# Block-sparse attention with a gated feed-forward: edge rows copied on chip, weights loaded behind the first inputs, squares added on GpSimd, fill matmuls, and new ranks

## The chip, the cores and the metric

The kernel runs on one core of a Trainium2 chip. The metric is the device time in microseconds (us), smaller is better. A core has five engines that run their own rows of instructions in order and wait for one another by semaphores: TensorE (PE in the profile, its weight loads apart as PEld), VectorE (DVE), ScalarE (ACT), GpSimd (POOL) and SyncE (SP, which here only issues transfers).

## The reference

Attention for 4 batches of 8 heads, 768 rows of 64 numbers each, and then a gated feed-forward over all 3072 tokens. Attention is sparse by blocks of 32 rows: a block of queries sees itself and its two neighbours, the first and the last block (the edge blocks), and three sampled blocks; the first and the last block of queries see all keys.

```python
scores = scale * np.matmul(q, k.transpose(0, 1, 3, 2))
mask = np.abs(blk_i - blk_j) <= window
mask = mask | (blk_i == 0) | (blk_j == 0) | (blk_i == n_blocks - 1) | (blk_j == n_blocks - 1)
...
        mask[qb * block:(qb + 1) * block, kb * block:(kb + 1) * block] = True
...
attn = attn / (np.sum(attn, axis=-1, keepdims=True) + 1e-09)
return np.matmul(attn, v).astype(np.float32)
```

```python
g = x @ w_gate
silu = g * (1.0 / (1.0 + np.exp(-g)))
val = x @ w_val
return (silu * val @ w_out).astype(np.float32)
```

Here x has 3072 rows of 512, w_gate and w_val are 512 x 1536, w_out is 1536 x 512.

## The kernel before

**Tiles and chunks.** A tile is four query blocks, 128 tokens; a batch has six. Tiles are grouped into nine chunks: three of two tiles (batch 0) and six of three tiles (batches 1 to 3). For each chunk the attention of its tiles writes x transposed into `xall`, and then `ffn_in` makes the hidden rows h, and `ffn_out` the output rows.

**Batch 0 and the weights.** The weights come as 64-bit words, in pieces of 512 KB, into four slots of `stage` (L453). VectorE turns two of them at a time into float32 by three passes (L431 to L433). Chunks 0 and 1 use those float32 weights (the "wide" projections, L1687). Meanwhile ScalarE and VectorE split each weight into two float16 halves (L391 and L394), and all later projections (`p`, L1693) and output matmuls (`po`, L1754) use three float16 products.

Batch 0's attention is worked in pairs of query blocks (`pair0`). A pair gathers its keys into `kring`, its values into a slot of `w2all`: window rows by copies from the resident v of batch 0 (L1315, on VectorE or ScalarE), sampled rows by an indirect transfer (L1319, issued by GpSimd), and edge rows, which four broadcast loads (L606) put once into all six slots, by `e0_done`. Then come scores (`qk`, L1338 and L1354), maxima on VectorE (`mx`, L1360), exponentials on ScalarE (`e`, L1371), transposes on TensorE (`pt`, L1379) with copies out (`pts`, L1385), the product with the values (`pv`, L1400), scaling (`xs`, L1408), a transpose back (L1417), and a copy into `xall` (L1464).

**The norm of a chunk.** `ffn_in` scales its hidden rows by a bound for the norm of x: ScalarE squares x (`sqx`, L1632) in four blocks of the chunk's tokens, four matmuls on a matrix of ones add them up over blocks and partitions (`xn`, L1637), and VectorE makes scales from it (L1641).

**What sets the order.** Nothing is ordered by hand. Each step is a task of a planner (`Plan.add`) with an engine, a cost in us, the tasks it needs, the buffers it takes, and a rank. `Plan.order` plays the tasks through: an engine that is free takes the task with the lowest rank of those that are ready and whose buffers are free by the planner's own clock. `queue` and `lanes` model the transfers. The ranks get an addition by key from the table `SHIFT`, thousands either way, so the table sets the order in fact. The tasks are then emitted in that order, so each engine's row is fixed when the program is built. `behind` puts a task behind another on its queue; `first_loads` chains the first loads on SP's queue. SP uses eight lanes for its transfers: a ninth waits for the one eight before it.

Of the kernel before, what the change touches and what calls it, by code (L numbers as in the profile page):

```python
# [13 lines left out]
ALU = mybir.AluOpType  # L14
AX = mybir.AxisListType

P = 128
B, H, S, D = 4, 8, 768, 64
BLK = 32
# [24 lines left out]
LANES = 8  # L44


SHIFT = {
# [72 lines left out]
class Plan:  # L120
# [9 lines left out]
    def add(self, eng, us, emit, need=(), rank=0.0, take=(), use=(), dma=None, behind=None, late=0.0, many=1):  # L130
# [8 lines left out]
        if behind is not None:  # L139
            behind.next.append(t)  # L140
# [87 lines left out]
def tile_block_sparse_attn_swiglu(  # L228
# [381 lines left out]
    def more_v0(rank):  # L610
        for i in range(1, 3):
            batches[0].v0_part(i, rank)
# [1240 lines left out]
```

## Time and profile before

Times are the median of three runs, 798.54 us (798.23 to 799.63). The profile shows one execution of its own.

| what | value |
|---|---|
| profiled execution | 799.88 us |
| its span, first to last instruction | 798.1 us |
| TensorE busy | 758.0 us (95%) |
| VectorE busy | 548.9 us (69%) |
| ScalarE busy | 507.5 us (64%) |
| GpSimd busy | 208.3 us (26%) |
| mean granted clock of TensorE | 0.991 |
| moved by transfers | 128.08 MB |

How to read it: the page gives the busy time of each engine and the span in 40 slices. The timeline lists instructions with start, duration and, in brackets, how long the engine was idle before and what released it. A row may stand for several instructions (x16). The table of stretches gives each engine's busy time between two points of the span; the stretch's length less that is the engine's idle. Idle time of an engine matters only where it holds up what ends last.

### The profile page before, as it was taken

Reading aid. Unit: us, or ns where it says so; the run is one execution under the profiler, and the core shown is the slowest. Engines: PE = TensorE matmul, PEld = TensorE weight load, DVE = VectorE, ACT = ScalarE, POOL = GpSimd, SP = SyncE. Lnnn points to the kernel's source line nnn. Section 1 sums busy time; section 2 is a strip of 40 time slices with the busy share of each in tenths; the row PEclk is TensorE's granted clock in tenths of the full one; section 3 lists DMA queues with packets and bytes.
Section 4 is the critical chain, followed back from the end, with each engine's and each line's share of the span. In section 5 each row is a group of like instructions: output and inputs, shape, how many; then the busy total and the mean of one; then the engine's idle time right before and its main releaser. Section 6 shows DMA issues by size and latency. Waiting matters only on the chain. (4 is left out here: it accounts for less than half of the span.)

```text
span 798.1 us, 21157 instructions
## 1 busy us (share of the span) xinstructions
PE 758.0 (95%) x8062; PEld 482.3 (60%) x8062; DVE 548.9 (69%) x1662; ACT 507.5 (64%) x1232; POOL 208.3 (26%) x257
## 2 busy tenths in 40 slices
PE   3689999999999999999999999999999999999998
PEld 2468778874687566645665566545665566555653
DVE  5688898997898696742799757654798767731320
ACT  2699657688688686754588746664497757642211
POOL 3466302322043232102233232301223233101210
PEclk9799999999999999999999999999999999999999
DMA  8965547558787977677779994947878974430001
GB/s 203 258 215 177 184 158 235 198 145 215 182 179 170 216 164 160 125 212 215 159 170 177 259 245 95 182 103 206 187 141 185 222 170 110 65 74 14 1 1 39
DMA packets 171286, 128.08 MB, mean 160 GB/s; under 512 B 114992, under 2 KB 136624, under 8 KB 171184
## 3 DMA queue, kind: packets, MB, share of 16 engines
q1 hardware_dynamic: 165552, 109.42, 57.2%
q0 software_dynamic: 5632, 17.31, 8.7%
q8 instruction: 63, 1.03, 0.6%
q14 instruction: 39, 0.32, 0.1%
HBM read 79.50 MB, written 11.01 MB: 113 GB/s over the span
## 5 line engine op out<-in xcount | busy, mean ns | idle before, releaser
L1693 PE MATMUL p<-xall,w1t 128*128 128x384 f16 (+1 forms) x2016 | 326.8, 319 | 0.0
L1693 PEld LDWEIGHTS <-w1t 128*128 128x128 f16 x2016 | 191.1, 98 | 116.1 <-issue 9.0
L1715 POOL TENSOR_TENSOR h<-act,h 128x384 f16<-128x384 f32 (+1 forms) x108 | 101.1, 937 | 375.7 <-ACT h L1712 375.4
L1754 PE MATMUL po<-w2all,h 128*128 128x512 f16 x864 | 195.2, 379 | 0.3 <-DVE w2all L394 0.3
L1754 PEld LDWEIGHTS <-h 128*128 128x128 f16 x864 | 81.0, 98 | 97.0 <-issue 5.7
L1121 POOL DMA_INDIRECT w2all<-vd,vidx x66 | 64.9, 983 | 150.3 <-PE pv L1203 127.6
L1702 DVE SCALAR_TENSOR_TENSOR act<-act,p 128x384 f32<-128x384 f32 (+1 forms) x108 | 54.2, 503 | 68.2 <-ACT act L1698 67.6
L1712 ACT CAST h<-act 128x384 f16<-128x384 f32 (+1 forms) x108 | 50.6, 470 | 78.5 <-DVE act L1707 78.2
L1687 PE MATMUL p<-xall,w1t 128*128 128x256 f32 x384 | 88.2, 383 | 1.3 <-DVE act L1702 1.3
L1165 ACT ACTIVATE e<-e,nb,es 128x256 f32<-128x256 f32 x132 | 78.2, 593 | 2.2
L1687 PEld LDWEIGHTS p<-xall,w1t 128*128 128x128 f32 x384 | 70.8, 190 | 12.7 <-DVE act L1702 1.9
L1698 ACT ACTIVATE act<-p,gsc 128x384 f32<-128x384 f32 (+1 forms) x84 | 46.9, 558 | 31.8 <-PE p L1693 31.3
L1203 PEld LDWEIGHTS <-w2all 128*128 128x128 f16 x1584 | 55.0, 98 | 16.1 <-issue 6.4
L1707 DVE SCALAR_TENSOR_TENSOR act<-act,hs,p 128x384 f32<-128x384 f32 (+1 forms) x84 | 49.6, 590 | 20.3 <-PE p L1693 17.7
L394 DVE SCALAR_TENSOR_TENSOR pp<-e,rr,pp 128x256 f16<-128x256 f32 x132 | 61.1, 510 | 1.3 <-ACT pp L391 1.0
L1203 PE MATMUL pv<-pts,w2all 128*128 128x64 f16 x1584 | 57.0, 193 | 4.6 <-DMA pts<-pp 3.2
L391 ACT ACTIVATE pp<-e,rr 128x256 f16<-128x256 f32 x132 | 58.1, 496 | 4.4 <-DVE rr L779 2.8
L1148 DVE CUSTOM_DVE_ANT_1 e<-qk,msk 128x256 f32<-128x256 f32 x132 | 49.9, 417 | 3.1 <-issue 2.7
L1593 ACT ACTIVATE ot<-po,oc 128x512 f32<-128x512 f32 x24 | 16.4, 683 | 44.1 <-PE po L1754 43.9
L1111 DVE COPY kring<-kst 128x256 f16 x198 | 38.7, 251 | 6.3 <-PE qk L1134 6.3
L1229 DVE TENSOR_TENSOR xall<-pv,xall 64x256 f16<-64x256 f32 x66 | 27.7, 420 | 21.1 <-ACT xall L1224 20.0
L1134 PE MATMUL qk<-kring,qs 128*32 128x256 f16 x1056 | 35.7, 274 | 0.8 <-DVE mx L1148 0.6
(189 smaller groups left out, 899.1 us busy)
## 6 DMA issues: line engine op xcount, KB each, us to landing
stage<-in_w_dram SPq DMA_DIRECT2D x36, 512.0 KB, 4.4
w2all<-vd SPq DMA_DIRECT2D x66, 192.0 KB, 3.9
qs<-qraw SPq DMA_DIRECT2D x72, 128.0 KB, 2.4
out_dram<-ot SPq DMA_DIRECT2D x20, 256.0 KB, 2.7
qn<-in_q_dram SPq DMA_DIRECT2D x36, 128.0 KB, 4.0
qraw<-in_q_dram SPq DMA_DIRECT2D x36, 128.0 KB, 3.1
stage<-in_v_dram SPq DMA_DIRECT2D x9, 512.0 KB, 5.3
vd<-stage SPq DMA_DIRECT2D x9, 512.0 KB, 5.9
```

Source lines behind the costliest of these rows:

```text
L391: nc.scalar.activation(hi, src, AF.Copy, scale=scale)
L394: nc.vector.scalar_tensor_tensor(lo, src, scale, hi, op0=ALU.mult, op1=ALU.subtract)
L1121: nc.gpsimd.indirect_dma_start(vf[0:96, 1, :], None, bt.vd, bass.IndirectOffsetOnAxis(ap=vidx[0:96, qb : qb + 1], axis=0))
L1148: nc.vector.tensor_tensor_reduce(ev[:, g], stv[:, g], o.g.msk[:, qb, :].unsqueeze(2).broadcast_to([P, 8, BLK]), scale=1.0, scalar=-3.0e38, ...
L1165: nc.scalar.activation(ev[:, g], ev[:, g], AF.Exp, bias=nb_[:, g : g + 1], scale=o.g.es[:, 0:1], accum_out=c["rs"][:, g : g + 1],)
L1203: nc.tensor.matmul(pvv[:, j, n % 2], vg[:, cc, l, 2 * j : 2 * j + 2, :], pq[:, g, m, cc, u : u + 2, :], start=i == 0, stop=i == 5,)
L1687: nc.tensor.matmul(t[:, 0:tc_], w[:, i + 1, k_ * P : (k_ + 1) * P], x_k(k_), start=k_ == 0, stop=k_ == NKT - 1)
L1693: nc.tensor.matmul(t[:, 0:tc_], w_[:, f, m, k_, :], x_k(k_, l), start=i == 0, stop=i == 11)
L1702: nc.vector.scalar_tensor_tensor(a_, a_, 1.0, pg.tile[:, 0:tc_], op0=ALU.add, op1=ALU.mult)
L1712: nc.scalar.copy(hv(f)[:, 0, :], act.tile[:, 0:tc_])
L1715: nc.gpsimd.tensor_tensor(hv(f)[:, 1, :], act.tile[:, 0:tc_], hv(f)[:, 0, :], op=ALU.subtract)
L1754: nc.tensor.matmul(po.tile, hv(f)[:, l, ts_], w2h[:, f, m, :], start=f == 0 and i == 0, stop=f == NF - 1 and i == 2)
```

## The change

Seven edits go together.

- The four broadcast loads of edge rows go. `edges` copies the first and the last 32 rows of v into the slots on chip: four copies of 32 x 512 on ScalarE, four of 32 x 1024 on VectorE. A pair's product needs the copies of its own slots (`edge_of`) in place of all four loads. The last part of v is loaded directly behind the first, the middle one later.
- Weight loads are chained behind the last of the first loads, not behind the seventh.
- The four blocks of squares are added on GpSimd, two on two and then one on one (`add_up`), and one matmul on ones is left of four.
- 83 tasks of four matmuls of ones by ones, 128 x 128 (`keep_on`), with rank 9000, so that the planner takes them when TensorE has nothing else that is ready. They write into the ring of buffers `pv`.
- The planner's prices: transfers start at 3.9 in place of 2.0 us, the table has no `late`, and early TensorE tasks get the price of later ones.
- Query loads and their spreading are chained in order (`q_last`).
- A new table `SHIFT`, with keys for the new copies.

```diff
+DMA_START = 3.9
...
-    "a0.0": 215.65, "a0.1": -2208.54, "a1.0": 2743.2, "a1.1": -905.98, "a2.0": -5449.96, "a2.1": 1137, "a3.0": -2069.74,
+    "a0.0": 2014.17, "a0.1": -1926.27, "a1.0": 1312.03, "a1.1": 3189.83, "a2.0": 3082.71, "a2.1": 1535.27, "a3.0":
...
-        a = add("SP", 0.37, lambda: load(0), need, rank, take=raw, behind=first_loads[6], dma=1.7)
+        a = add("SP", 0.37, lambda: load(0), need, rank, take=raw, behind=first_loads[-1], dma=1.7)
...
         part(0, rank)
-        for m in range(2):
-            sl = slice(0, BLK) if m else slice(96, P)
-            for n, r0 in enumerate((0, S - BLK)):
-                e0_done.append(first(add("SP", 0.45, lambda m=m, sl=sl, n=n, r0=r0: nc.sync.dma_start(
-                    w2all[sl, n + 2 * m : 2 * V0_RING : 4, :],
-                    v[0, r0 : r0 + BLK, :].unsqueeze(1).broadcast_to([BLK, V0_RING // 2, DM])), [], rank, behind=first_loads[-1], dma=0.8)))
+        part(2, rank)
+
+    def edges(x, n, k, eng, us, rank):
+
+        sl = slice(0, BLK) if x % 2 else slice(96, P)
+        src = w2t[96:P, V0_AT + NTB - 1, :] if n else w2t[0:BLK, V0_AT, :]
+
+        def copy():
+            f = nc.vector.tensor_copy if eng == "DVE" else nc.scalar.copy
+            f(w2all[sl, 2 * x + n : 2 * x + n + 4 * k - 3 : 4, :], src.unsqueeze(1).broadcast_to([BLK, k, DM]))
+
+        plan.key = f"e{x}.{n}"
+        t = add(eng, us, copy, [batches[0].v0_loads[2 * n]], rank)
+        batches[0].v0_read.append(t)
+        for i in range(x, x + 2 * k, 2):
+            edge_of[i].append(t)
+
+    def all_edges(rank):
+        for x in range(2):
+            for n in range(2):
+                edges(x, n, 1, "ACT", 0.62, rank)
+        for x in range(2, 4):
+            for n in range(2):
+                edges(x, n, 2, "DVE", 0.7, rank + 0.5)
...
-        a = in_turn("pv", "PE", 1.06 if ci else 1.8, product, there + vl + e0_done, rank, take=[pv], use=pts)
+        a = in_turn("pv", "PE", 1.06, product, there + vl + [t for x, _ in vb for t in edge_of[x]], rank, take=[pv], use=pts)
...
-            for j in range(4):
-                nc.tensor.matmul(t[:, 0:tc_], ones_h, sq_view()[:, j], start=j == 0, stop=j == 3)
+            nc.tensor.matmul(t[:, 0:tc_], ones_h, sq_view()[:, 0], start=True, stop=True)
+
+        def add_up(n):
+            x = sq_view()
+            nc.gpsimd.tensor_tensor(x[:, 0:n], x[:, 0:n], x[:, n : 2 * n], op=ALU.add)
...
-        a = add("PE", nt * 0.22, norms, [a], rank - 1000.0, take=[xn], use=[sq])
+        a = add("POOL", 0.64 * nt, lambda: add_up(2), [a], EVAC, use=[sq])
+        a = add("POOL", 0.32 * nt, lambda: add_up(1), [a], EVAC, use=[sq])
+        a = add("PE", nt * 0.055, norms, [a], rank - 1000.0, take=[xn], use=[sq])
...
+    def keep_on(n, us):
+        plan.key = ""
+
+        def turn_over(w):
+            t = get(w, "idle")
+            for _ in range(4):
+                nc.tensor.matmul(t[:, 0:P], ones_h, ones_h, start=True, stop=True)
+
+        for _ in range(n):
+            w = Buf("pv")
+            add("PE", us, lambda w=w: turn_over(w), [t_id], 9000.0, take=[w])
...
+    keep_on(8, 0.43)
+    keep_on(75, 0.21)
     load_k0(K0)
```

In the changed program the 332 fill matmuls stand on TensorE as follows: 100 ahead of the first transposes of k, 28 between them, 60 behind them and ahead of the first scores, and 144 between scores, transposes and products of the pairs up to the sixth.

On SP's queue at the start of the program, before: query tile 0 (`q_0`), the first part of v, the edge rows (32x3x512), a weight piece (`stage`), query tile 1, and the rest.

```order
L1265 DMA q_0_132<-in_q_dram 64x4x128 x2
L597 DMA w2all<-in_v_dram 128x2x512
L606 DMA w2all<-in_v_dram 32x3x512 x4
L453 DMA stage<-in_w_dram 128x1024
L1265 DMA q_0_132<-in_q_dram 64x4x128 x2
L597 DMA w2all<-in_v_dram 128x2x512 x2
L453 DMA stage<-in_w_dram 128x1024 x3
L1265 DMA q_1_459<-in_q_dram 64x4x128 x4
```

The same place on SP's queue now:

```order
L1289 DMA q_0_147<-in_q_dram 64x4x128 x2
L600 DMA w2all<-in_v_dram 128x2x512 x2
L1289 DMA q_0_147<-in_q_dram 64x4x128 x2
L600 DMA w2all<-in_v_dram 128x2x512
L1289 DMA q_1_473<-in_q_dram 64x4x128 x4
L456 DMA stage<-in_w_dram 128x1024 x4
```

The edge loads are gone, the second query tile moved ahead of one v part and of the first weight piece, and chunk 1's queries (`q_1`) ahead of all weights.

On ScalarE's row behind the copies of k's transposes, where it first needs v, before: window copies into `w2all`, the squares of v (`vsq`), then the exponentials of the first pair (`nb_1`, `e_1`).

```order
L1315 COPY w2all<-w2all 96x512
L1315 COPY w2all<-w2all 64x512
L1315 COPY w2all<-w2all 32x512
L398 ACTIVATE vsq_361,vacc_360<-w2all 128x1024
L1315 COPY w2all<-w2all 96x512
L1369 ACTIVATE nb_1_0_419<-mx_1_376 128x2
L1371 ACTIVATE e_1_0_417,rs_1_416<-qk_1_0_321,nb_1_0_419 128x256 x2
```

The same place on ScalarE's row now, with the edge copies (L615):

```order
L615 COPY w2all<-w2all 32x512
L401 ACTIVATE vsq_589,vacc_588<-w2all 128x1024
L615 COPY w2all<-w2all 32x512 x2
L401 ACTIVATE vsq_589,vacc_588<-w2all 128x1024
L1393 ACTIVATE nb_1_0_679<-mx_1_626 128x2
L1395 ACTIVATE e_1_0_677,rs_1_676<-qk_1_0_549,nb_1_0_679 128x256 x2
L1339 COPY w2all<-w2all 96x512
```

Three edge copies and a second part of v's squares, which needs the second v load, moved ahead of the first pair's exponentials, and the window copies behind them.

On GpSimd's row near the end, where the last chunk's h begins (`h_0`), before: the last differences of the chunk before it, and then those of the last chunk.

```order
L1715 TENSOR_TENSOR h_8_11627<-act_9_11652,h_8_11627 128x384
L1715 TENSOR_TENSOR h_10_11762<-act_10_11723,h_10_11762 128x384
L1715 TENSOR_TENSOR h_10_11762<-act_11_11813,h_10_11762 128x384
L1715 TENSOR_TENSOR h_0_12209<-act_0_12192,h_0_12209 128x384
L1715 TENSOR_TENSOR h_0_12209<-act_1_12225,h_0_12209 128x384
```

The same place on GpSimd's row now:

```order
L1744 TENSOR_TENSOR h_8_12076<-act_9_12107,h_8_12076 128x384
L1744 TENSOR_TENSOR h_10_12257<-act_10_12195,h_10_12257 128x384
L1744 TENSOR_TENSOR h_10_12257<-act_11_12313,h_10_12257 128x384
L1664 TENSOR_TENSOR sqx_12490<-sqx_12490 128x768
L1664 TENSOR_TENSOR sqx_12490<-sqx_12490 128x384
L1744 TENSOR_TENSOR h_0_12619<-act_0_12602,h_0_12619 128x384
```

The two adds of squares stand between the two chunks' differences, and TensorE's one norm matmul waits for the second of them.

More of the change, by code (lines that the diff above doesn't have):

```diff
@@ L137, in add @@
         t.outs, t.next, t.ready, t.end, t.no = [], [], 0.0, None, len(self.tasks)
-        t.left = len(t.need) + (behind is not None)
-        if behind is not None:
-            behind.next.append(t)
+        behind = behind if isinstance(behind, list) else [behind] * (behind is not None)
+        t.left = len(t.need) + len(behind)
+        for x in behind:
+            x.next.append(t)
         for x in t.need:
@@ L171, in order @@
                 waiting[t.eng].append(t)
-        queue = 2.0
+        queue = DMA_START
         lanes = [0.0] * LANES
@@ L369, in tile_block_sparse_attn_swiglu @@
     t_pre = add("DVE", 1.5, before, [], rank=-250.0)
-    t_tab = add("DVE", 0.75, tables, [first(add("SP", 0.4, load_tab, rank=-400.0, dma=0.4, late=1.2)), t_pre], rank=-200.0)
+    t_tab = add("DVE", 0.75, tables, [first(add("SP", 0.4, load_tab, rank=-400.0, dma=0.4)), t_pre], rank=-200.0)
     t_rep = add("DVE", 2.0, repeats, [t_tab], rank=TAB)
@@ L580, in keep @@
                     k0_of()[:, :, t * P : (t + 1) * P], kp.tile.rearrange("p (j t) -> p j t", j=4))
-            a = add("PE", 0.9, turn, [loads[t // 2], t_id], rank, take=[kp])
+            a = add("PE", 0.47, turn, [loads[t // 2], t_id], rank, take=[kp])
             bt.k_turned.append(a)
@@ L593, in load_v0 @@
         v0 = w2t[:, V0_AT : V0_AT + NTB, :]
[L594 removed]
+        bt.v0_loads = [None] * 3
         def part(i, rank):
[L597 removed]
+            bt.v0_loads[i] = first(add("SP", 0.45, lambda i=i: nc.sync.dma_start(
                 v0[:, 2 * i : 2 * i + 2, :], v[0, i * 256 : (i + 1) * 256, :].rearrange("(t p) n -> p t n", p=P)),
[L599 removed]
+                [], rank, behind=first_loads[-1], dma=2.0))
         bt.v0_part = part
         part(0, rank)
[L603 to L608 removed]
+        part(2, rank)
[17 more added lines that the diff above has]
+                edges(x, n, 2, "DVE", 0.7, rank + 0.5)
     def more_v0(rank):
[L611 to L612 removed]
+        batches[0].v0_part(1, rank)
     def norm_v0(rank):
@@ L762, in tile_block_sparse_attn_swiglu @@
     v_first = [[] for _ in range(V0_RING)]
-    e0_done = []
+    edge_of = [[] for _ in range(V0_RING)]
     sparse_no = [0]
@@ L875, in spread @@
             o.q = q_.rearrange("p t l j q -> p l j t q")
-        need = [g.scaled, add("SP", 1.27, load, [], rank, behind=g.loaded, take=hold, dma=1.6, many=2)]
+        need = [g.scaled, add("SP", 1.27, load, [], rank, behind=[g.loaded] + q_last[0:1], take=hold, dma=1.6, many=2)]
+        loaded = need[1]
         t = add("ACT", 0.63, lambda: hi_part(two()[:, 0, :], raw_q(), g.siq[:, 0:1]), need, rank, use=hold)
         t = add("DVE", 0.67, lambda: lo_part(two()[:, 1, :], raw_q(), g.siq[:, 0:1], two()[:, 0, :]), [t], rank, use=hold)
-        o.done = add("SP", 2.4, spread, [t], rank, take=[qs], use=hold, dma=2.4, many=4)
+        o.done = add("SP", 2.4, spread, [t], rank, behind=q_last[1:], take=[qs], use=hold, dma=2.4, many=4)
+        q_last[:] = [loaded, o.done]
         return o
@@ L1436, in pair0 @@
                   use=[bt.ks, o.regbuf]) for i in range(2)]
-        s = in_turn("qk", "PE", 1.4 if ci else 2.2, scores, kc + [o.done, t_rep], rank, take=qk, use=[o.qs, bt.ks])
+        s = in_turn("qk", "PE", 1.4, scores, kc + [o.done, t_rep], rank, take=qk, use=[o.qs, bt.ks])
         for i in range(2):
@@ L1444, in pair0 @@
         for hh in range(2):
-            a = in_turn("turn", "PE", 0.47 if ci else 0.8, lambda hh=hh: turn(hh), [x_[hh], t_id], rank, take=[pt[hh]], use=[e[hh]])
+            a = in_turn("turn", "PE", 0.47, lambda hh=hh: turn(hh), [x_[hh], t_id], rank, take=[pt[hh]], use=[e[hh]])
             there.append(in_turn(f"turned{hh}", *(("DVE", 0.6) if hh and not ci else ("ACT", 0.47)), lambda hh=hh: turned(hh), [a], rank,
```

8 lines of the change are left out of this document (4 added, 4 removed), and 107 rows, old and new, of the table SHIFT.

## The prediction

> **What bounds the kernel now.** I read the page's table of engines and its slices first, then the busy times by stretch, then the timeline of the start, then single groups for prices. The page:
>
> ```profile
> PE 758.0 (95%) x8062; PEld 482.3 (60%) x8062; DVE 548.9 (69%) x1662; ACT 507.5 (64%) x1232; POOL 208.3 (26%) x257
> PEclk9799999999999999999999999999999999999999
> ```
>
> TensorE (PE) works 758.0 of the span's 798.1 us, and only its first two slices show a lower granted clock. So the question is where its 40 us of idle lie, and what ends them. The table of stretches (start and end in us, length, then busy us of each engine):
>
> ```profile
> core 0: us, PE busy (x) PEld busy (x) DVE busy (x) ACT busy (x) POOL busy (x), PEclk, DMA share, GB/s
> 0.00:17.30 17.30, 7.07 (x132) 5.68 (x139) 8.87 (x44) 3.04 (x5) 5.08 (x12) 1.00 0.83 207
> 17.30:57.40 40.10, 27.73 (x752) 18.95 (x740) 29.21 (x64) 33.28 (x97) 21.41 (x45) 0.83 0.84 228
> 57.40:140.00 82.60, 80.72 (x1099) 65.44 (x1098) 73.40 (x170) 60.30 (x161) 28.46 (x41) 1.00 0.58 192
> 140.00:177.00 37.00, 34.91 (x165) 29.96 (x164) 35.19 (x76) 28.86 (x58) 10.07 (x10) 1.00 0.54 171
> 177.00:724.00 547.00, 537.31 (x5541) 323.61 (x5540) 388.18 (x1288) 366.22 (x887) 132.34 (x140) 1.00 0.75 168
> 724.00:798.10 74.10, 70.29 (x397) 38.64 (x395) 14.03 (x24) 15.84 (x28) 10.95 (x12) 1.00 0.05 15
> ```
>
> TensorE idles 10.2 us before 17.3, 12.4 us from there to 57.4, 1.9 + 2.1 us up to 177, 9.7 us up to 724, and 3.8 us at the end (the last scaling and store). So three things count: when TensorE gets continuous work (57.4), how much work it then has, and the holes behind that. Note the two stretches between 57.4 and 177: VectorE (DVE) idles only 9.2 and 1.8 us there, so it is nearly as full as TensorE. What paces the start:
>
> ```profile
> 4.33 0.84 SPq L597 DMA_DIRECT2D w2all<-in_v_dram  x1
> 5.21 4.43 SPq L606 DMA_DIRECT2D w2all<-in_v_dram  x4
> 11.41 0.35 SPq L453 DMA_DIRECT2D stage<-in_w_dram  x1
> 12.30 1.67 SPq L1265 DMA_DIRECT2D q<-in_q_dram  x2
> 17.30 1.87 ACT L1315 COPY w2all<-w2all 96x512 f32<-96x512 f32 x3 [4.51 <-DMA w2all<-in_v_dram]
> 27.20 0.75 PE L1338 MATMUL qk<-kst,q 64*32 64x96 f32 x9 [2.77 <-DMA q<-in_q_dram]
> 55.26 0.37 ACT L1464 COPY xall<-pv 128x256 f32<-128x256 f32 x1
> 57.54 3.62 PE L1687 MATMUL p<-xall,w1t 128*128 128x256 f32 x16
> ```
>
> ScalarE (ACT) waits for the first part of v until 17.3, TensorE for the second query tile until 27.2. At 55.26 ScalarE copies the last piece of chunk 0 out, and at 57.54 TensorE starts the wide projections. Between 17.3 and 55.26 ScalarE is busy 31.2 of 38.0 us (33.28 less the 2.1 it works from 55.26 to 57.4): it is the nearest to a bound there, with 6.8 us idle.
>
> **The change, part by part.** *Edge rows and order of the loads.* Ahead of the second query tile in SP's queue stand now four edge loads of 192 KB and one weight piece of 512 KB, 1.28 MB; in the change one more v part, 0.52 MB. At the stretch's 228 GB/s the 0.76 MB less are 3.3 us: the tile lands near 23.9 instead of 27.2. The v part that the lower edge rows are copied from follows the first one at once: 0.52 MB, 2.3 us, so 19.6. Batch 0's third and fourth query tiles move ahead of all weights. By the same rate the first weight pair (1.05 MB, 4.6 us) then lands near 33, and its decode stands behind the maxima of pair 9 in VectorE's row, which come here today:
>
> ```profile
> 45.13 1.29 DVE L1360 TENSOR_REDUCE mx<-qk 128x2 f32<-128x512 f32 x2 [0.24 <-PE qk L1354]
> ```
>
> Even if those come 6 us sooner, the weights are there, so their later loading costs nothing; with that cover gone it would cost up to one pair, 4.6 us.
>
> The copies go to ScalarE (four of 32 x 512) and VectorE (four of 32 x 1024):
>
> ```profile
> L1315 ACT COPY w2all<-w2all 32x512 f32<-32x512 f32 x7 | 4.3, 617 | 0.1
> L1315 DVE COPY w2all<-w2all 64x512 f32<-64x512 f32 x4 | 1.8, 460 | 0.1
> ```
>
> 4 x 0.617 = 2.5 us on ScalarE, and 4 x 2 x 0.460 = 3.7 us on VectorE. ScalarE then has 31.2 + 2.5 = 33.7 us to do from 17.3 to chunk 0's last copy. With no idle at all that copy would come at 51.0; with today's 6.8 us at 57.8. The earlier queries and v remove the two waits for loads that stand behind most of that idle; the wait for the second v part (19.6) puts back about 1 us. I take 3 us of idle: the copy comes at 54.0, 1.3 us earlier. Pair 9's product, which now stands directly before the first wide projection, follows within about 1.2 us; today 2.3 us lie between. So TensorE starts at 55.1 instead of 57.5: **-2.4 us**, with ends of -5 and +2.
>
> *What VectorE takes back.* From 57.4 on it has no room to be shifted: its 3.7 us more are partly covered by its 8.4 us of idle before 17.3 and 10.9 us before 57.4, but they lie where v arrives, when it is busy. TensorE can only use its earlier start if VectorE's 11.0 us of idle up to 177 shrink. I give back a third: **+0.8 us**, ends 0 and +2.5.
>
> *Fill matmuls.* 332 of them, 128 x 128. No row has one. The nearest:
>
> ```profile
> 451.83 0.70 PE pv L1203 x24
> 457.51 0.65 PE xn L1637 x4
> 7.70 3.44 PE L574 MATMUL kT<-ident,w1t 128*128 128x128 f32 x16 [7.70 <-DVE dup L356]
> 11.53 1.07 PE L574 MATMUL kT<-ident,w1t 128*128 128x128 f32 x8 [0.39 <-DMA w1t<-in_k_dram]
> ```
>
> 24 of 64 columns take 0.70 us (0.029 each), 4 of 384 columns 0.65 us (0.1625 each), so 128 columns take about 0.054. 188 of them stand before the first scores: 10.2 us, exactly the idle of the first 17.3 us. The transposes of k cost 0.215 us each at the start and 0.134 later, so the first fills may run at half speed, and the first hundred (5.4 us, or up to 10.8) may reach past the 7.7 us at which k is there, by up to 4 us. Behind that lie the wait for v until 17.3 and faster transposes (16 x 0.08 = 1.3 us back). 144 more (7.8 us) stand between scores and products up to pair 11, where ScalarE paces. I cost them at nothing: the cover is TensorE's 12.4 us of idle up to 57.4. The last 44, behind pair 7's scores, cost 2.4 us if TensorE has no idle there. A steady clock (0.83 in that stretch) shortens TensorE's links of the chain; that is inside my 3 us of idle.
>
> *One norm matmul for four.* Removed: 3 in each of 9 chunks, six of 384 columns and three of 256:
>
> ```profile
> 152.65 0.60 PE L1637 MATMUL xn<-sqx,ones_h 128*128 128x256 bf16 x4
> 153.09 1.89 PE L1687 MATMUL p<-xall,w1t 128*128 128x256 f32 x8
> ```
>
> Four of 256 columns fill 152.65 to 153.09, 0.11 each. 18 x 0.1625 + 9 x 0.11 = 3.9 us, all on TensorE's full path: **-3.9 us**. Added are two adds on GpSimd (POOL), of 2 and 1 blocks of a chunk's tokens:
>
> ```profile
> L1715 POOL TENSOR_TENSOR h<-act,h 128x384 f16<-128x384 f32 x72 | 68.2, 947 | 250.3 <-ACT h L1712 250.1
> L1715 POOL TENSOR_TENSOR h<-act,h 128x256 f16<-128x256 f32 x36 | 32.9, 917 | 125.4 <-ACT h L1712 125.3
> ```
>
> By these, 3 x 0.947 = 2.8 us in a chunk of three tiles and 3 x 0.917 = 2.75 us in one of two: 25 us on an engine that is 26% busy. The matmul stands in TensorE's row and waits for them, with all projections queued behind it. The last chunk today:
>
> ```profile
> 711.71 4.05 PE L1754 MATMUL po<-w2all,h 128*128 128x512 f16 x18
> 711.91 0.74 ACT L1224 CAST xall<-pv 64x256 f16<-64x256 f32 x2 [4.60 <-PE pv L1203]
> 712.68 1.48 ACT L1632 ACTIVATE sqx<-xall 128x1536 bf16<-128x1536 f16 x1
> 715.59 0.81 PE L1637 MATMUL xn<-sqx,ones_h 128*128 128x384 bf16 x4
> ```
>
> Squares end at 714.2, 2.5 us after the product; with 2.8 us of adds and their hand-overs the sum is there 5.6 us after it. In the change 36 output matmuls (twice the 18 that fill 711.71 to 715.59, so 7.8 us) stand between. That covers it by 2.2 us. Elsewhere the planner's own prices (1.92 + 0.96) agree with the row, but gathers and other adds queue ahead on GpSimd, so I give back **+0.7 us**, ends 0 and +6.
>
> *GpSimd against VectorE.* The two disturb each other here:
>
> ```profile
> 139.31 1.15 POOL L1715 TENSOR_TENSOR h<-act,h 128x256 f16<-128x256 f32 x1 [1.36 <-ACT h L1712]
> 139.85 1.16 DVE L431 TENSOR_SCALAR w2all<-stage 128x1024 int32<-128x1024 int32 x1
> 150.77 0.68 DVE L431 TENSOR_SCALAR w2all<-stage 128x1024 int32<-128x1024 int32 x1
> ```
>
> The same VectorE step takes 1.16 us beside a GpSimd add and 0.68 alone. The Trainium skill (page "SBUF — State Buffer", section "Who interferes with whom") says that a VectorE instruction with two SBUF inputs, or in a 2-port mode, locks GpSimd's port pair or is locked out by it for the whole instruction; taken whole, that makes the 8.3 us of adds of the first three chunks time lost to VectorE, an estimate of 801.8 us. The rows agree that something waits, but 0.48 us for an add of 1.15, so 0.42 of it; by them it is rival A.
>
> *New ranks and queue rules elsewhere.* They reorder everything. The row of TensorE after has the same work otherwise, and 36 projections of chunk 2 stand ahead of batch 1's first scores. I find nothing that forces the 9.7 us of holes from 177 to 724 to shrink or grow: 0, ends -5 and +5.
>
> Sum: -2.4 + 0.8 - 3.9 + 0.7 = -4.8, rounded to -5 us with the steadier clock. The profiled execution took 799.88 us (span 798.1), 1.34 above the median of 798.54; I take the difference over: **793.5 us**.
>
> **Rivals.** *A, VectorE is the bound (0.14).* For: 1.8 us of idle in 37 us up to 177. Against: 9.2 us in the stretch before. Then the 2.4 us are lost whole, and the first three chunks' adds (3 x 2.75 = 8.3 us) stop VectorE for 0.42 of their time, +3.5; with -3.9 it gives 798.1. The lock that the Trainium skill's page "SBUF — State Buffer" describes would work in this way.
>
> *B, slower: TensorE waits for the adds (0.10).* One place in each chunk: the norm matmul. If an add takes 1.7 times its price, as 1.15 against the group's shortest 0.67 shows, a chunk's sum comes 2 us later, and what other work does not cover is lost on TensorE. For a mean of 1.2 us over nine chunks: 798.5 - 1.6 - 3.9 + 10.8 = 803.8. It decides from a mean of 0.8 us on. Against it: the cover of 7.8 us in three chunks, and that no xn matmul waits today.
>
> *C, the new order closes holes (0.15).* Half of the 9.7 us: 788.7.
>
> *D, the fills do not do what they say (0.05).* The clock is no steadier, and the last 44 fall where TensorE is late: +2.4, 795.9.
>
> **How the numbers follow.** The forecast has 0.56, with its own range of 790 to 797. 0.2% of 798.5 is 1.6 us, about what a measurement tells from no change: faster is below 796.9, slower above 800.1. Faster: nearly all of the forecast (0.54), C (0.15), part of D and the low side of A (0.06): 0.75. Slower: B and the forecast's worst end: 0.11. The same: 0.14. The range from 787.5 to 799.5 takes in C, A and D and leaves out B and C's far end.
>
> **What would show it.** Right: q's second tile ends TensorE's wait near 24 us, ScalarE's copy of chunk 0 near 54, wide projections from about 55, one norm matmul a chunk without idle before it, a clock of 1.0 up to 57. Wrong: idle before the norm matmul released by GpSimd (B); VectorE without idle up to 177 and TensorE waiting for its results (A); less or far more than 9.7 us of holes between 177 and 724 (C, or an order that is worse); scores or products that come late behind fill matmuls (D).

## The result, and the profile after

The changed kernel takes 810.25 us (median of four runs, 806.69 to 811.14), the kernel before 799.09 beside it. The ratio is **1.0133** (95%: 1.0104 to 1.0163): slower by 1.3%, about 10.6 us, where I forecast 793.5 us and gave 0.11 to slower. The profiled execution of the changed kernel took 809.91 us, its span 808.1. One later profile, that of after_same_chip, fell on a slow execution and is not used.

Page of the changed kernel, busy time of the engines and granted clock in 40 slices:

```profile
PE 774.2 (96%) x8367; PEld 499.3 (62%) x8367; DVE 560.8 (69%) x1666; ACT 511.9 (63%) x1236; POOL 231.6 (29%) x275
PEclk9899999999999999999999999999999999999999
```

TensorE is busier by 16.2 us than before (758.0), and VectorE by 11.9 us (548.9) though it has only four instructions more (1666 against 1662), the edge copies of 0.7 us each. The other 9 us of VectorE come back below.

The same stretches as before, of the changed kernel:

```profile
core 0: us, PE busy (x) PEld busy (x) DVE busy (x) ACT busy (x) POOL busy (x), PEclk, DMA share, GB/s
0.00:17.30 17.30, 16.23 (x265) 16.10 (x269) 9.40 (x44) 5.32 (x8) 2.97 (x10) 1.00 0.84 233
17.30:57.40 40.10, 32.12 (x820) 25.98 (x805) 26.72 (x61) 30.30 (x91) 21.73 (x45) 0.91 0.70 189
57.40:140.00 82.60, 78.59 (x1200) 62.63 (x1200) 74.21 (x159) 61.14 (x160) 34.74 (x45) 1.00 0.53 177
140.00:177.00 37.00, 35.80 (x168) 30.51 (x167) 35.49 (x84) 26.71 (x56) 12.21 (x12) 1.00 0.52 171
177.00:724.00 547.00, 531.42 (x5497) 321.02 (x5496) 399.55 (x1290) 371.90 (x895) 149.05 (x154) 1.00 0.79 171
724.00:808.10 84.10, 80.02 (x443) 43.04 (x440) 15.38 (x31) 16.55 (x29) 10.94 (x12) 1.00 0.05 16
```

Two places lost, the start and the stretch from 177 to 724. From 17.3 to 57.4 ScalarE, which paces the start, idles 9.8 us (before 6.8) and VectorE 13.4 (before 10.9), while TensorE looks fuller: the fill matmuls. And from 177 to 724 TensorE idles 15.6 us, before 9.7. Counted from the first wide projection to the end, first of the kernel before, then of the changed one:

```profile
57.54:798.10 740.56, 723.09 (x7196) 457.51 (x7194) 510.65 (x1556) 471.08 (x1132) 181.68 (x202) 1.00 0.65 156
60.25:808.10 747.85, 723.01 (x7175) 455.05 (x7169) 523.27 (x1559) 473.48 (x1133) 205.79 (x218) 1.00 0.67 154
```

The wide projections start 2.7 us later. TensorE's work behind that takes the same 723 us, though 21 matmuls fewer stand there, and its idle grows from 17.5 to 24.8 us. Together this is the 10.0 us between the two spans.

The start, from the timeline of the changed kernel (start, duration, engine, line, what; in brackets the idle time before and what ended it):

```profile
14.15 0.62 ACT L615 COPY w2all<-w2all 32x512 f32<-32x512 f32 x1 [0.66 <-DMA w2all<-in_v_dram]
16.59 0.40 PE L1362 MATMUL qk<-kst,q 64*32 64x96 f32 x16
17.57 0.62 ACT L615 COPY w2all<-w2all 32x512 f32<-32x512 f32 x1 [1.11 <-DMA w2all<-in_v_dram]
...
22.29 0.20 ACT L1395 ACTIVATION_READ_ACCUMULATOR e<-qk,nb 128x1 f32 x1
24.12 0.32 PE L1362 MATMUL qk<-kst,q 64*32 64x96 f32 x1 [3.90 <-issue]
25.35 2.77 PE L1801 MATMUL idle<-ones_h 128*128 128x128 bf16 x24
27.91 1.06 PE L1403 MATMUL pt<-ident,e 128*128 128x128 f32 x4
29.01 0.59 ACT L1409 COPY pts<-pt 128x512 f32<-128x512 f32 x1 [6.52 <-PE pt L1403]
58.22 0.40 ACT L1488 COPY xall<-pv 128x256 f32<-128x256 f32 x1
60.25 1.99 PE L1716 MATMUL p<-xall,w1t 128*128 128x256 f32 x8
```

Read it from ScalarE. Its first exponentials end at 22.5, and then it stands for 6.52 us until a transpose comes out of TensorE. TensorE stops for 3.90 us, up to 24.12, in the middle of the second block of scores, for nothing that the profile shows ("issue"). Then it runs 24 fills at about half speed (2.77 us at a granted clock of 0.50; the same 24 take 1.50 elsewhere), ahead of the transposes that ScalarE waits for. The copy that ends chunk 0 begins at 58.22 (before 55.26), the wide projections begin at 60.25 (before 57.54).

What TensorE waited for in the whole span, some of the groups of waits of the changed kernel (sum, times, longest):

```profile
PE pv L1227 <- DMA pts<-pp: 6.3, 5, 2.9
PE qk L1362 <- issue: 5.0, 3, 3.9
PE nrm_k L391 <- ACT stage L401: 3.2, 2, 2.1
PE qk L1158 <- DVE mx L1172: 3.0, 7, 0.7
PE xn L1660 <- POOL sqx L1664: 0.6, 1, 0.6
```

And of the kernel before:

```profile
PE pv L1203 <- DMA pts<-pp: 3.2, 4, 1.3
PE nrm_k L388 <- ACT stage L398: 2.2, 2, 1.3
PE qk L1134 <- DVE mx L1148: 0.6, 2, 0.4
PE qk L1338 <- issue: 0.6, 1, 0.6
```

Transposed probabilities (`pts`), norms of k and maxima all come later against TensorE's row. For GpSimd's adds it waits once, for 0.6 us: rival B did not happen.

### The profile page after: what moved, and what is told of

Same layout as the page of the kernel before. It is cut to its first block, busy times and chain, and to the rows that moved or that the text cites. A ratio compares the mean times of both kernels' runs of the same rounds, so it can differ in the third digit from the quotient of the medians.

```text
span 808.1 us, 21752 instructions
## 1 busy us (share of the span) xinstructions
PE 774.2 (96%) x8367; PEld 499.3 (62%) x8367; DVE 560.8 (69%) x1666; ACT 511.9 (63%) x1236; POOL 231.6 (29%) x275
## 3 DMA queue, kind: packets, MB, share of 16 engines
q8 instruction: 65, 1.06, 0.5%
## 5 line engine op out<-in xcount | busy, mean ns | idle before, releaser
L1617 ACT ACTIVATE ot<-po,oc 128x512 f32<-128x512 f32 x24 | 16.4, 683 | 54.8 <-PE po L1783 47.0
L1135 DVE COPY kring<-kst 128x256 f16 x198 | 41.4, 267 | 4.4 <-PE qk L1158 3.8
L1253 DVE TENSOR_TENSOR xall<-pv,xall 64x256 f16<-64x256 f32 x66 | 27.7, 420 | 18.2 <-ACT xall L1248 16.2
```

## The experiments

Theories: F, the fills cost time at the start; G, the adds on GpSimd cost more than the three matmuls save; O, the new order opens holes; C, the edge copies pace the start. All ratios are to the kernel before, run beside each kernel on the same chip; four chips served for these. Its executions scatter there by up to 1.7%, so only ratios with their intervals are compared, and two ratios that lie 0.3 to 0.4% apart are not told apart. A profile shows one execution: those of no_fill and fill_noadd are the fastest of their kernels and those of fill_wide and norm4 the slowest, each 0.6 to 0.75% off the median, so spans of profiles are not compared.

| kernel | ratio (95%) | wide projections start at |
|---|---|---|
| changed | 1.0133 (1.0104 to 1.0163) | 60.25 |
| no_fill | 1.0059 (1.0038 to 1.0081) | 54.73 |
| fill_wide | 1.0065 (1.0039 to 1.0091) | 58.45 |
| fill_early | 1.0091 (1.0065 to 1.0116) | 58.46 |
| fill_late | 1.0114 (1.0080 to 1.0149) | 57.70 |
| fill_narrow | 1.0148 (1.0117 to 1.0178) | 62.30 |
| norm4 | 1.0126 (1.0088 to 1.0163) | 62.29 |
| no_fill_norm4 | 0.9981 (0.9953 to 1.0008) | 55.32 |
| no_fill_noadd | 0.9989 (0.9959 to 1.0019) | 56.74 |
| no_fill_adds_apart | 1.0053 (1.0029 to 1.0077) | 52.91 |
| fill_noadd | 1.0090 (1.0056 to 1.0124) | 59.41 |
| fill_wide_norm4 | 1.0084 (1.0052 to 1.0117) | 58.99 |
| edge_dma | 1.0193 (1.0165 to 1.0221) | 66.12 |
| before_edges | 1.0009 (0.9988 to 1.0029) | 57.84 |
| before_xn | 1.0211 (1.0170 to 1.0252) | 58.23 |
| before_late_new | 1.0228 (1.0199 to 1.0257) | 57.06 |
| no_fill_late_old | 1.0301 (1.0268 to 1.0333) | 55.73 |
| no_fill_same_chip | 1.0051 (1.0025 to 1.0077) | 54.43 |
| after_same_chip | 1.0155 (1.0115 to 1.0194) | – |

### The fill matmuls

**no_fill.** The planner's tasks stay, so every row keeps its order; nothing is issued for them.

```diff
         def turn_over(w):
-            t = get(w, "idle")
-            for _ in range(4):
-                nc.tensor.matmul(t[:, 0:P], ones_h, ones_h, start=True, stop=True)
+            return
```

> The changed kernel with the same order of everything, but its 332 fill matmuls on ones are not issued (nothing of the result depends on them). Theory F (the fills cost time at the start): TensorE's second block of scores stops there from 19.9 to 24.12 without a semaphore, 2.5 us after which a 16 KB packet of the instruction queue had begun, and the 48 fills behind it run at half clock (2.77 and 1.99 us) between the exponentials and the transposes. Without them the wide projections start at 54 to 56 instead of 60.2, and the time falls by 4 to 6 us, to 804 to 806. Theory O (the new ranks cost it: holes of 15.6 us instead of 9.7 between 177 and 724, and the start is set by ScalarE and VectorE): the wide projections start at 59 to 60 and the time stays at 809 to 811.

Measured: 1.0059, 0.7% less than the changed kernel, about 6 us; theory F. Timeline of the kernel without fills:

```profile
11.35 0.43 PE L1362 MATMUL qk<-kst,q 64*32 64x96 f32 x16
13.62 0.79 PE L1362 MATMUL qk<-kring,q 64*32 64x160 f32 x16 [1.84 <-DVE kring L1322]
18.74 0.86 PE L1403 MATMUL pt<-ident,e 128*128 128x128 f32 x4
54.73 1.99 PE L1716 MATMUL p<-xall,w1t 128*128 128x256 f32 x8
```

The first scores begin at 11.35 instead of 16.59, the first transposes come at 18.74 instead of 27.91, and the wide projections at 54.73: 5.5 us earlier than with the fills.

**fill_wide, fill_early, fill_late, fill_narrow.** Which fills, and what of them? In the same order: a quarter of the instructions for the same columns; the first 188 or the last 144 alone; all 332 with 2 columns.

```diff
-            for _ in range(4):
-                nc.tensor.matmul(t[:, 0:P], ones_h, ones_h, start=True, stop=True)
+            nc.tensor.matmul(t.rearrange("p (a b) -> p a b", a=4), ones_h, ones_h.unsqueeze(1).broadcast_to([P, 4, P]), start=True, stop=True)
```

```diff
+            no_fill[0] += 1
+            if no_fill[0] - 1 >= 47:
+                return
             t = get(w, "idle")
```

```diff
-                nc.tensor.matmul(t[:, 0:P], ones_h, ones_h, start=True, stop=True)
+                nc.tensor.matmul(t[:, 0:2], ones_h, ones_h[:, 0:2], start=True, stop=True)
```

(The second is fill_early; fill_late has `< 47`.)

> The changed kernel with each group of four fill matmuls of 128 columns issued as one of 512 columns: the same columns, 83 matmuls and weight loads instead of 332. Theory F in its form 'instruction supply': the stop of 3.9 us in the second block of scores is gone or under 1 us, because TensorE reaches its next block of instructions later; the wide projections start at 55 to 57.5 and the time is 805 to 808. Theory F in its form 'the fills' own time': the stop may go, but the fills still stand between scores and transposes, and the start of the wide projections stays at 59 to 60, the time at 809 to 811.

> The changed kernel in the same order with only the first 188 fill matmuls, those ahead of the first scores. Theory 'instruction supply': it is these that bring TensorE early to the end of the instructions that it has, in the stretch in which the loads fill the DMA queues; a stop of 2 us or more in the scores stays, the wide projections start at 58 or later, and the ratio is 1.010 to 1.013. Theory 'the late fills' own time' (they stand between scores and transposes, 48 of them at half clock): the wide projections start at 55 to 56.5 and the ratio is 1.005 to 1.008.

> The changed kernel in the same order with only the last 144 fill matmuls, those behind the first scores. Theory 'instruction supply': the wide projections start at 55 to 56.5, ratio 1.005 to 1.008. Theory 'the late fills' own time': they start at 58 or later, ratio 1.010 to 1.013.

> The changed kernel in the same order with all 332 fill matmuls, each of 2 columns instead of 128: the same instructions, little of TensorE's time. With 332 full fills the ratio was 1.0133, without any 1.0059, with the same columns in a quarter of the instructions 1.0065. Theory 'instructions': it is their number that costs, so the ratio stays at 1.010 to 1.014. Theory 'time of the fills': 1.005 to 1.008.

Measured: 1.0065, 1.0091, 1.0114, 1.0148. Early and late fills each seem to cost a part (0.3 and 0.55% above no_fill, give or take 0.3 and 0.4%), so neither of the two theories that I set against each other has it alone. With the same columns in a quarter of the instructions the cost was nearly gone in total (1.0065 against 1.0059 on the same chip), which speaks for the number of instructions. Fills with a sixty-fourth of the columns cost as much as full ones, but this does not rule the fills' own time out. The group of fills in the changed kernel and in fill_narrow:

```profile
L1801 PE MATMUL idle<-ones_h 128*128 128x128 bf16 x332 | 25.1, 241 | 1.1 <-DVE ones_h L302 1.1
L1801 PE MATMUL idle<-ones_h 128*128 128x2 bf16 x332 | 14.1, 165 | 3.4 <-remote 1.9 <-DVE ones_h L302 1.1 <-PE idle L1801 0.4
```

The narrow ones still hold TensorE for 14.1 us, against 25.1, and the granted clock from 17.3 to 57.4 fell to 0.74 beside them (0.91 beside the full ones), which slows what stands between them. And fill_wide still started its wide projections at 58.45, and with four norm matmuls (below) its fills cost 1.0%. So the split between the fills' place in the row, their time and their number of instructions stays open. What is the same in all: the eight kernels with fills and the start of the change begin the wide projections at 57.7 to 62.3, the six without fills at 52.9 to 56.7.

### The norm

**norm4** puts the four matmuls back and drops the adds, in the same order; **no_fill_norm4** does that without the fills.

```diff
-            nc.tensor.matmul(t[:, 0:tc_], ones_h, sq_view()[:, 0], start=True, stop=True)
+            for j in range(4):
+                nc.tensor.matmul(t[:, 0:tc_], ones_h, sq_view()[:, j], start=j == 0, stop=j == 3)
...
         def add_up(n):
-            x = sq_view()
-            nc.gpsimd.tensor_tensor(x[:, 0:n], x[:, 0:n], x[:, n : 2 * n], op=ALU.add)
+            return
```

> The changed kernel in the same order, with the four norm matmuls per chunk of the kernel before, and without the two adds on GpSimd. By the prediction's price for that part (-3.9 on TensorE, +0.7 for waits) the time rises by about 3 us, to 813. If the adds cost TensorE more than they save (rival B, or VectorE is held up by them), it falls, to 807 to 809. The trace shows only one wait of 0.6 us for an add, so I expect 812 to 814.

> The changed kernel in the same order without the fill matmuls (which nothing depends on) and with the four norm matmuls per chunk in place of the two adds and one matmul; to be compared with the same kernel without this (ratio 1.0059). If the norm part is worth the 3.2 us net that the prediction gave it: 1.009 to 1.011. If it is worth nothing here: 1.004 to 1.008.

Measured: 1.0126 against 1.0133, no difference where I expected 3 us; and without the fills 0.9981 against 1.0059, the opposite of what I expected: the norm part of the change costs 0.7 to 0.8%. My price (-3.2 us) falls. Three more kernels split it: one matmul and no adds (no_fill_noadd, fill_noadd: `add_up` returns at once); adds that nobody waits for, beside four matmuls (no_fill_adds_apart).

```diff
+    apart = const.tile([P, 384], BF16, name="apart")
...
-            nc.gpsimd.tensor_tensor(x[:, 0:n], x[:, 0:n], x[:, n : 2 * n], op=ALU.add)
+            for i in range(n):
+                nc.gpsimd.tensor_tensor(apart[:, 0:tc_], x[:, i], x[:, n + i], op=ALU.add)
```

> The changed kernel in the same order without fill matmuls and without the adds on GpSimd, with one norm matmul per chunk, which so sums only the first of four blocks of squares: the saving on TensorE by itself. Against the same with four matmuls (0.9981) the prediction's 3.9 us would give 0.993 to 0.994. If the order leaves nothing to be gained by 27 matmuls fewer, because TensorE then waits for others by as much: 0.997 to 1.000.

> The changed kernel in the same order without fill matmuls, with four norm matmuls, and with the adds still made on GpSimd (as three of one block each, into an area that nobody reads): their load on GpSimd and on what shares its memory ports or queue, with nobody waiting for them. Against 0.9981 without them: if the adds by themselves cost the 6 us that lie between the kernels with and without the norm part, 1.003 to 1.008; if they cost only by TensorE's wait for their sum, 0.997 to 1.000.

The kernel without fills and the changed kernel ran unchanged beside them:

> The changed kernel without the fill matmuls once more, on the chip of the two kernels before: 1.004 to 1.008 if the difference of 0.8% to the kernel with four norm matmuls is one of the kernels; 0.997 to 1.001 if it was one of the chips.

> The changed kernel itself, on the same chip: 1.010 to 1.016 if the fill matmuls cost 0.7% as between the first runs; 1.004 to 1.008 if that was a difference of chips.

Measured on one chip: 0.9989 without adds, 1.0053 with adds that nobody waits for, 1.0051 with adds in use, 1.0155 with the fills too. So the adds cost 0.6%, 5 us, merely by running, and the 27 matmuls saved gain nothing without the fills (0.9981 to 0.9989, where 3.9 us would be 0.5%). The pages of the profile say where the adds act, first without them (no_fill_noadd), then with them apart (no_fill_adds_apart):

```profile
PE 759.7 (95%) x8035; PEld 481.6 (60%) x8035; DVE 549.1 (69%) x1666; ACT 512.1 (64%) x1236; POOL 209.7 (26%) x257
```

```profile
PE 759.5 (95%) x8062; PEld 482.6 (60%) x8062; DVE 558.4 (70%) x1666; ACT 511.9 (64%) x1236; POOL 233.8 (29%) x284
```

And one of the groups of VectorE that grow, in the same two kernels (busy us, mean ns of one): the low halves of the queries of batches 1 to 3.

```profile
L397 DVE SCALAR_TENSOR_TENSOR qraw<-qraw,siq 128x512 f16<-128x512 f32 x18 | 13.6, 753 | 5.5 <-ACT qraw L394 5.2
```

```profile
L398 DVE SCALAR_TENSOR_TENSOR qraw<-qraw,siq 128x512 f16<-128x512 f32 x18 | 15.4, 854 | 6.1 <-ACT qraw L395 5.8
```

The same 1666 instructions of VectorE take 9.3 us longer beside 24.1 us of adds: 0.39 of their time. The pair no_fill_norm4 and no_fill shows the same (549.1 and 559.0). This is the mechanism that the prediction weighed as rival A, at the price that it read from one row (0.42), but in all nine chunks.

The single instructions show how. Here are three adds of no_fill_adds_apart with VectorE's work beside and behind them, and a step on the queries beside three others:

```profile
454.90 3.08 POOL L1667 TENSOR_TENSOR apart<-sqx 128x384 bf16<-128x384 bf16 x3 [0.80 <-ACT sqx L1657]
455.71 1.22 DVE L1136 COPY kring<-kst 128x256 f16 x3 [1.35 <-PE qk L1159]
457.21 0.42 DVE L1173 CUSTOM_DVE_ANT_1 e<-qk,msk 128x256 f32<-128x256 f32 x1
457.91 0.49 DVE L1136 COPY kring<-kst 128x256 f16 x3
...
526.40 1.40 DVE L398 SCALAR_TENSOR_TENSOR qraw<-qraw,siq 128x512 f16<-128x512 f32 x1
```

Three copies take 1.22 us beside the adds and 0.49 when the adds are over; the step on the queries takes 1.40 us where it takes 0.75 alone; the maxima (0.42, their mean without adds too) lose nothing. The adds wait as well: three of this size take 3.55 us beside the step on the queries and 2.89 with VectorE idle (from 525.01 and from 710.09). The Trainium skill (page "SBUF — State Buffer", section "Who interferes with whom") says that a VectorE instruction with two SBUF inputs contends with a GpSimd instruction that reads SBUF, that one in a 2-port mode contends too, and that the engine which comes first keeps the shared ports for its whole instruction. The trace agrees: an add of this size takes 0.91 us undisturbed (at 710.09), and the copies and the step on the queries lose 0.73 and 0.65 us. The 0.39 is an average in which some adds meet no such instruction and others meet one for a part of their time.

How the 9.3 us reach TensorE: from the first wide projection to the end, without adds (no_fill_noadd) and with adds in use (no_fill_same_chip), one chip and the same instructions of TensorE and VectorE:

```profile
56.74:797.10 740.36, 724.00 (x7171) 455.97 (x7169) 510.49 (x1557) 472.00 (x1128) 182.22 (x197) 1.00 0.67 156
54.43:798.20 743.77, 722.48 (x7171) 455.44 (x7169) 519.85 (x1557) 471.14 (x1128) 207.05 (x214) 1.00 0.66 155
```

VectorE works 9.4 us longer, and TensorE idles 21.3 us in place of 16.4: 4.9 us, near the 5 us of the ratios. no_fill_norm4 idles 16.4 there too, no_fill 21.1 and no_fill_adds_apart 20.3. The added idle is spread over several groups of waits, none of which makes it alone. That it all comes by way of VectorE is argued and not shown: GpSimd's gathers also stand behind the adds in its row. TensorE waits directly for no gather and no difference of GpSimd in these kernels, but a way over ScalarE was not tested.

> The changed kernel with all its fill matmuls, without the adds on GpSimd, with one norm matmul per chunk, which so sums only the first of four blocks of squares. If the adds cost 0.6% with the fills as they do without (1.0051 against 0.9989): 1.007 to 1.010. If the fills hide that cost, as four matmuls in place of the adds suggested (1.0126 against 1.0133): 1.012 to 1.016.

> The changed kernel with the fills as 83 matmuls of 512 columns and with four norm matmuls and no adds. If both costs add up (adds 0.6%, number of fill instructions 0.7%), neither is left: 0.997 to 1.001. If the adds cost nothing where fills are, 1.004 to 1.008.

Measured: 1.0090, so taking the adds from the changed kernel with all its fills gains 0.4 to 0.65%, as without fills. But fill_wide_norm4, at 1.0084, did not fall to 1.0 with both costs away, and came out just above where I had put it if adds cost nothing beside fills. The two do not fit together, and that stays open. With fills, four matmuls cost 0.36% more than one (1.0126 against 1.0090, on two chips), near my 3.9 us but within the intervals, and without them nothing. So the saving of the matmuls is somewhere from 0 to 0.4%; the intervals (some 0.3% each way) do not allow more.

**before_xn** has the norm part alone in the old order, the adds placed behind the squares, where the planner had left no room for them.

```diff
             nc.scalar.activation(sq_view(), ..., AF.Square)
+            x = sq_view()
+            for n in (2, 1):
+                nc.gpsimd.tensor_tensor(x[:, 0:n], x[:, 0:n], x[:, n : 2 * n], op=ALU.add)
...
-            for j in range(4):
-                nc.tensor.matmul(t[:, 0:tc_], ones_h, sq_view()[:, j], start=j == 0, stop=j == 3)
+            nc.tensor.matmul(t[:, 0:tc_], ones_h, sq_view()[:, 0], start=True, stop=True)
```

> The kernel before, in its own order, with only the norm part of the change: two adds on GpSimd right behind each chunk's squares, one norm matmul instead of four. If the prediction's price holds (27 matmuls fewer, 18 x 0.1625 + 9 x 0.11 = 3.9 us, less 0.7 for waits) the ratio to the kernel before is 0.996. If the saving is taken back elsewhere (TensorE busy 723.1 us behind the start both before and after the change, and four norm matmuls put back made no difference that could be measured), the ratio is 0.999 to 1.001. If TensorE waits for the adds (rival B), it is over 1.002, with waits for sqx in the trace.

Measured: 1.0211. Its waits of TensorE:

```profile
PE xn L1639 <- POOL sqx L1635: 10.9, 6, 3.4
PE pv L1203 <- DMA pts<-pp: 8.4, 8, 2.4
```

Here rival B does happen, six times. The changed kernel, whose planner had a place for the adds, waits 0.6 us in all.

### The start and the order

**edge_dma** loads the edge rows behind the third v part, as the kernel before did, instead of copying them. **before_edges** is the opposite: the old order with the new start (copies; the third v part directly behind the first; the first weight piece behind the second query tile).

```diff
             def load(i=i):
                 nc.sync.dma_start(v0[:, 2 * i : 2 * i + 2, :], ...)
+                for m in range(2 if i == 2 else 0):
...
+                        nc.sync.dma_start(w2all[sl, n + 2 * m : 2 * V0_RING : 4, :],
+                                          v[0, r0 : r0 + BLK, :].unsqueeze(1).broadcast_to([BLK, V0_RING // 2, DM]))
...
         def copy():
+            return
```

> The changed kernel in the same order, with the edge rows of v loaded by four DMAs of 192 KB behind the third v part, as the kernel before loads them, instead of the eight copies on ScalarE and VectorE. Theory 'the copies pace the start': ScalarE is rid of 2.5 us and VectorE of 2.8 us, the wide projections start 1 to 2 us earlier, time 808 to 809. Theory 'loads pace the start', as in the prediction's -2.4: all query tiles land 3.3 us later and the wide projections start up to 3 us later, time 810 to 813.

> The kernel before in its own order, with the start's part of the change alone: edge rows copied on ScalarE and VectorE instead of loaded four times, the third v part directly behind the first, the first weight piece behind the second query tile. The prediction's first two terms (-2.4 and +0.8) give a ratio of 0.998, with the second query tile's scores at about 24 instead of 27.2 us and the wide projections from 55 instead of 57.5. If what stands behind cannot use the earlier start, or the copies delay the first maxima, it is 1.000 to 1.004.

Measured: 1.0193 with the wide projections at 66.12, 5.9 us later than in the changed kernel, twice what I expected at most. So 0.77 MB of loads in place of the copies delay the start more than the copies do, and the copies are not what makes the change slow (theory C falls). What each weighs alone this kernel does not show, since it changes both. And 1.0009: in the old order the new start gains nothing; chunk 0's last copy comes at 52.61 (before 55.26), the wide projections still start at 57.84.

**before_late_new** gives the kernel before the new numbers for 144 steps of chunks 4 to 8; **no_fill_late_old** gives the kernel without fills the old ones there.

```diff
-    "a4.0": 5700.15, "a4.1": 484.53, "a4.2": 1104.53,
+    "a4.0": -179.29, "a4.1": 529.45, "a4.2": 6544.61,
...
```

(And so for every key a, b, o and p of chunk 4 and up; the other kernel has the signs the other way round.)

> The kernel before with the changed kernel's numbers for 144 of the 351 steps (attention, projections and outputs of chunks 4 to 8); the order of TensorE's row is the same for its first 2690 of 12483 rows, and the work is the same throughout. If an order is worth up to 5 us either way (theory O, the holes of 15.6 us against 9.7 between 177 and 724 in the changed kernel), the ratio leaves 1 by 0.004 or more, with longer waits of TensorE for the transposed probabilities, the maxima or the norms. If orders are worth nothing, as the prediction took it, it is 0.998 to 1.002.

> The changed kernel without the fill matmuls (which nothing depends on), with the kernel before's numbers for 144 steps of chunks 4 to 8; TensorE's row is the same for its first 1506 of 12428 rows. If the new numbers make the late stages worse as such, the old ones there bring the ratio from 1.0059 down to 1.000 to 1.003. If a set of numbers fits only the kernel that it belongs to, as the opposite exchange showed (1.0228), it rises to 1.012 or more.

Measured: 1.0228 and 1.0301, with the same work. Waits of before_late_new, and the stretches around the longest (length, TensorE busy, granted clock, share and rate of the transfers):

```profile
PE pv L1203 <- DMA pts<-pp: 15.2, 10, 6.0
```

```profile
440.00:460.00 20.00, 19.27 (x295) 1.00 1.11 240
460.00:480.00 20.00, 12.74 (x118) 0.66 0.84 181
480.00:500.00 20.00, 19.98 (x216) 1.00 0.66 137
```

Exchanging part of the table cost 2 to 3%, and a table fits only the kernel that it belongs to. Whether the new table is a worse one than the old, each in its own kernel, can't be told from these two. The holes of TensorE from 177 to 724 say more: 8.8 us in no_fill_norm4 and in no_fill_noadd, which have the new table with neither fills nor adds, 9.7 before. The new order by itself opens none (theory O falls). With adds they are 11.9 to 12.4, and 15.6 with the fills too.

**A version that beats both?** no_fill_norm4, the change without fills and without the norm part, is the fastest here: 0.9981 (0.9953 to 1.0008), faster than the changed kernel by 1.5% and not told apart from the kernel before. So none here is shown to beat both.

## Why the prediction was wrong, by its own steps

Three terms of the sum failed: the fills at 0 (measured +6 to +8 us), the adds at +0.7 (+5), and the norm matmuls at -3.9 (0 to -3). The two terms of the start are not contradicted.

- **Loads.** Right, and by more: TensorE waits for no query tile, the third v part is used from 17.57 (I said 19.6), and the first v part from 14.15 instead of 17.3, with the edge loads gone from behind it. I did not move that last one, though the 17.3 was the cover of a later step.
- **Start, -2.4 and +0.8.** Right in size in the new order: without fills the wide projections start at 52.9 to 56.7 (I said 55.1), and no_fill_norm4, which is these two terms and the order, stands at -0.2% (-0.5 to +0.1), I said -1.6 us. In the old order the same start gained nothing (before_edges, 1.0009, wide projections at 57.84), so the gain is not the start's alone, and -0.2% is not told apart from none.
- **Fill matmuls at 0: the step that failed.** I named as cover "TensorE's 12.4 us of idle up to 57.4". They cost 0.7% by no_fill and 1.0% on one chip, 6 to 8 us. They are also longer than I took them for: 25.1 us, where I had 10.2 and 7.8. And idle of a stretch is no cover for what stands in the row ahead of the scores and the transposes: those belong to the chain that ScalarE waits for. The cover of the first 188, the wait for v until 17.3, was taken away by the change itself. My bounds (+4 and +2.4) were nearer than my value, and I took the value below both. That the fills cost time, and delay the start, is shown by leaving them out; which property of theirs does it stays open.
- **Norm matmuls, -3.9: not gained.** The 27 matmuls saved 0 without the fills (0.9981 to 0.9989) and 0.36% with them, within the intervals, so between 0 and 3 us.
- **Waits for the adds, +0.7: right (0.6), and beside the point.** The adds cost 5 us without TensorE waiting for them, and lengthen VectorE's work by 9.3 us. I had this as rival A, priced it at 3.5 us for three chunks, and gave it 0.14, since VectorE "idles 9.2 us"; with all nine chunks in it and the matmuls' gain gone it would have come out slower than the kernel before. My 0.42 agrees with the average of 0.39 by luck: the add of 1.15 us that I read it from was itself lengthened, the shortest of its group takes 0.67.
- **Ranks at 0 (ends of 5).** The holes from 177 to 724 grew by 5.9 us. With the start of the change and the new order but neither fills nor adds the holes are 8.8 us (9.7 before) and the time is that of the kernel before, so 0 for the order alone is not contradicted, and the growth comes with the adds and the fills. By the exchanges a table that does not fit could have cost 20 us, so my ends were too narrow, and that it came out at 0 is luck.

Summed by ratios: -0.2% (start and order), +0.6% (adds), 0 to -0.4% (matmuls), +0.7 to 1.0% (fills): +0.7 to +1.4% for 1.33% measured. With intervals of about 0.3% on each part the sum is no finer than that.

## What to carry to other kernels

An instruction that does nothing costs nothing only if no one waits for what stands behind it in its engine's row: read the cover from the chain at that place, not from the idle time of the stretch, and ask whether the same change takes the cover away. Before work is moved to an idle engine, compare the busy time of the others for the same number of instructions: GpSimd was 26% busy and VectorE paid. And where a planner's table sets the order, part of a change can't be priced by leaving the rest of the order at zero: an exchanged table moved the time by 2 to 3%.

## What the runs showed of the hardware that I had not expected

- **TensorE stops without a releaser.** The traces have queues of instruction packets. In the changed kernel, from 21 to 22 us (packets, MB, share of the engines):

```profile
q8 instruction: 1, 0.02, 9.0%
```

  The stop of 3.90 us has no releaser and ends at 24.12, some 2.7 us behind the start of that packet, in a stretch in which the transfers' share is 1.06 (20 to 24.12). In the kernel without fills packets at 19, 26 and 31 us are followed by such stops (0.94 us, 1.53 and 0.15), and before there was one at 32 us with a stop of 0.60 ending at 34.82, but also one at 22 us with none. I take it that TensorE had no instructions; the trace does not say for which engine a packet is. Up to 62 us these stops sum to 2.7 to 6.6 us in the kernels with the new start, but also to 2.8 and 4.0 in before_late_new and before_xn with the old one (0.6 before): they are not the change's alone, and no run took them away. The Trainium skill (page "Runtime: NRT & Kernel Launch", section "Instruction fetch mechanics") calls the cost of crossing a 16 KiB boundary of instructions mostly hidden; if these stops are that, it was not hidden here, and no run tests it.
- **This wait of TensorE cost more than its length.** Around the wait of 6.0 us of before_late_new the granted clock is 0.66 in the 20 us from 460 (1.00 on both sides). The products behind the wait, and the same 24 ten us later:

```profile
466.11 1.44 PE L1203 MATMUL pv<-pts,w2all 128*128 128x64 f16 x24 [6.02 <-DMA pts<-pp]
476.41 0.86 PE L1203 MATMUL pv<-pts,w2all 128*128 128x64 f16 x24
```

- **Full fills raised the clock, and time was lost all the same.** From 17.3 to 57.4 the granted clock was 0.83 before, 0.83 to 0.96 in the six kernels without fills, 0.91 in the changed kernel and 0.91 to 1.00 with all or part of the fills of 128 or 512 columns (1.00 with 83 of 512), but 0.74 with fills of 2 columns. A steadier clock did not bring the wide projections forward.
